# Moving sums from GpSimd to VectorE and multiplying one token tile plainly, in a Mamba-2 and mixer kernel

## The chip, the core and the metric

The kernel runs on one core of a Trainium2 chip. The core has a matrix engine (TensorE, "PE" in the profile; its weight loads are "PEld"), three engines for elementwise work (VectorE "DVE", ScalarE "ACT", GpSimd "POOL"), and SyncE ("SP"), which here only issues DMA transfers. The engines run side by side, each works through its own instructions in program order, and they wait for each other by semaphores. The metric is the device time of one execution in microseconds.

## The reference

Two blocks follow each other. The first is a chunked state-space recurrence over 4 batches, 8 heads, 768 tokens, head width 32 and state width 16. The second mixes tokens with a rank-32 product and channels with a two-layer network of width 1024.

```python
# first block: per chunk c of 32 tokens
cum = np.cumsum(la, axis=-1)
L = np.exp(cum[:, :, :, None] - cum[:, :, None, :]) * causal
M = np.einsum('bhin,bhjn->bhij', Cc, Bc) * L
y_intra = np.einsum('bhij,bhjd->bhid', M, xc)
y_inter = np.einsum('bhin,bhnd->bhid', Cc, state) * np.exp(cum)[:, :, :, None]
y[:, :, sl] = y_intra + y_inter
Bx = np.einsum('bhjn,bhjd->bhjnd', Bc, xc) * decay_from_j[:, :, :, None, None]
state = decay_full[:, :, None, None] * state + np.sum(Bx, axis=2)
# heads are joined to (batch, 768, 256), then the second block
h = x.transpose(0, 2, 1) @ U @ V
u = x + h.transpose(0, 2, 1)
out = u + np.maximum(u @ w_ch1, 0.0) @ w_ch2      # w_ch1: 256 x 1024, w_ch2: 1024 x 256
```

The weights of the second block come as 64-bit floats and everything else as 32-bit floats.

## The kernel before

The tokens of a batch are taken as 6 blocks of 128, two blocks at a time: a *pair* k is two blocks of 128 tokens, and there are 12 pairs, 3 for each batch. All matrix products are fp32; the profile shows each as two TensorE passes.

For a pair the first block of the reference runs in these steps. `prep` scales B and C on VectorE into `BC`; `decayed` scales B on GpSimd into `bd`; `turn` transposes `BC` on TensorE and ScalarE copies it out; `gram` forms C times B, `mask` applies the causal mask on VectorE, `state` and `update` carry the state on (TensorE, VectorE, and GpSimd for `Sm`), `intra` and `inter` form y, `yout` copies it out, and `ytokens` transposes it into token order.

```python
def prep(k, c=0, n=2):
    ...
    nc.vector.tensor_tensor(out=st[k]["BC"]..., in0=bc_sb[k]..., in1=F..., op=ALU.mult)

def decayed(k, c=0, n=2):
    ...
    nc.gpsimd.tensor_tensor(out=st[k]["bd"]..., in0=bc_sb[k]..., in1=FD..., op=ALU.mult)

def ytokens(k, c, n):
    ...
    copy = nc.scalar.copy if b == 0 else nc.vector.tensor_copy
    behind.setdefault("part", copy(out=ytok[b]..., in_=t))
```

The weights arrive as pairs of 32-bit words and are turned into fp32 by `to_fp32`, whose five VectorE and two ScalarE operations are spread out by calls of `convert_ahead`.

PSUM tiles come from `bank`; where TensorE would otherwise stand idle, `fill(n)` asks the next `bank` for n products of the identity with itself, whose result is overwritten, and `warm(n)` does the same at the start.

```python
def bank(tag, *dims):
    t = psum.tile([P, *dims], FP32, tag=tag, name=tag, bufs=BANKS[tag])
    for _ in range(fills[0]):
        ...
        nc.tensor.matmul(out=flat[:, :n], lhsT=ident, rhs=ident[:, :n], start=True, stop=True)
    fills[0] = 0
    return t
```

In the mixer of batch 0 the first product of the channel network is plain (`up`: one 128-column slice m of w_ch1 for one half k of the tokens, 384 columns wide). In the other batches it runs in *quads*: seven products instead of eight for each 2x2 split, with sums of the operands (`t` and `ws`) and of the results.

The second product is done in `down(j)` for j = 0, 1, 2, each for two tiles of 128 tokens, in all batches with seven groups of 128-column products. It needs four sums of gT, formed in `sums`, and sums of the weights, `w2s`, formed by `operands`.

```python
def sums(lo=0, hi=NM // 2, which=range(4)):
    ...
    for v, (l, r, op) in enumerate((
            (A21, A22, ALU.add), (S[0], A11, ALU.subtract),
            (A11, A21, ALU.subtract), (A12, S[1], ALU.subtract))):
        if v in which:
            engine = nc.gpsimd if b and j == 0 and lo < 3 else nc.vector
            engine.tensor_tensor(out=S[v][:, lo:hi], in0=l[:, lo:hi], in1=r[:, lo:hi], op=op)

def times(name, tag, lhsT, rhs, start=True, u=None):
    ...
    for i in range(NM // 2):                       # four products of 128 columns
        nc.tensor.matmul(out=X[name], lhsT=lhsT[:, i], rhs=rhs[:, i], ...)

def p1(): ...; times("x", "x", blocks()[0][0], w2b[0][0]); kept("e", "x")
def p5(): times("y", "z", S[0], w2s[0]); kept("power", "y")
# p6, p3, p7, p2, p4: the other five; `added` joins two results on VectorE into o, `store` sends o off

work = [(w2s[0], w2b[0][1], w2b[0][0], ALU.subtract), ...,     # 4 of w2s
        (ws[:, 0], A[2], A[3], ALU.add), ...]                  # 4 of ws
def operands(n, engine):
    for _ in range(min(n, len(work))):
        out, l, r, op = work.pop(0)
        engine.tensor_tensor(out=out, in0=l, in1=r, op=op)     # 128 x 512 each
```

The order in which the pieces of the mixer are interleaved with the pairs is written out by hand:

```python
for _ in range(3):
    some(2)                    # two up products
    convert_ahead()
decays(others, "y"); keep(others)
prep(3); decayed(3)
some(2)
turn(3); convert_ahead()
some(2)
gram(3); state(3); mask(3); update(3)
prep(4); decayed(4)
some(2)
turn(4); convert_ahead()
plan[0].append(convert_ahead)
...
for k in range(NPR, last + 1):                     # NPR = 3
    b, q = divmod(k, NPR)
    pieces = plan[q] if q or b == 1 else []        # mixer of the batch before
    if k > NPR:
        tokens = [lambda: ytokens(k - 1, 0, 2)]
        if q:
            pieces = pieces[:4] + tokens + pieces[4:]
        else:
            late = downs
            project, mixed, ups, plan, downs, _ = mixer(b - 1)
            pieces = (late[:1] + tokens + late[1:7] + [project] + late[7:11] + [mixed]
                      + late[11:] + (plan[0] if k < last else []))
    ...
    prep(k + 2); decayed(k + 2)
    run(pieces)
    turn(k + 2)
    inter(k, 0); gram(k + 1); intra(k); state(k + 1); mask(k + 1); inter(k, 1); yout(k)
    update(k + 1)
    if k == NPR + 1:
        run(ahead)                                 # the four sums of batch 0, j = 0
    if k < 2 * NPR:
        operands((2, 2, 4)[k - NPR], nc.gpsimd)
```

`plan[q]` for batch 0 is: two up products; two up products; the seven groups of j = 0 and the sums for j = 1.

Of the kernel before, what the change touches and what calls it, by code (L numbers as in the profile page):

```python
# [20 lines left out]
def kernel(  # L21
# [27 lines left out]
    nc = tc.nc  # L49
# [26 lines left out]

    def bank(tag, *dims):
        t = psum.tile([P, *dims], FP32, tag=tag, name=tag, bufs=BANKS[tag])
        for _ in range(fills[0]):
            flat = t if len(dims) == 1 else t.rearrange(  # L80
                {2: "p a b -> p (a b)", 3: "p a b c -> p (a b c)"}[len(dims)])
            n = min(P, flat.shape[1])
            nc.tensor.matmul(out=flat[:, :n], lhsT=ident, rhs=ident[:, :n], start=True, stop=True)
        fills[0] = 0
        return t
# [126 lines left out]
    def warm(n, tag="w"):  # L212

        t = bank(tag, P)
        for _ in range(n):
            nc.tensor.matmul(out=t, lhsT=ident, rhs=ident, start=True, stop=True)  # L216
# [307 lines left out]

    def mixer(b):
# [123 lines left out]
        def down(j):  # L649
# [7 lines left out]
            def sums(lo=0, hi=NM // 2, which=range(4)):  # L657
# [8 lines left out]
                for v, (l, r, op) in enumerate((  # L666
                        (A21, A22, ALU.add), (S[0], A11, ALU.subtract),
                        (A11, A21, ALU.subtract), (A12, S[1], ALU.subtract))):
                    if v in which:
                        engine = nc.gpsimd if b and j == 0 and lo < 3 else nc.vector  # L670
                        engine.tensor_tensor(out=S[v][:, lo:hi], in0=l[:, lo:hi],  # L671
                                             in1=r[:, lo:hi], op=op)
# [73 lines left out]

            return sums, [p1, p5, p6, p3, p7, p2, p4]
# [5 lines left out]
        def step(j, v, lo=0, hi=NM // 2):  # L753
            return lambda: sums[j](lo, hi, (v,))
# [26 lines left out]
        return project, mixed, ups, plan, downs, [step(0, v) for v in range(4)]  # L781
# [32 lines left out]
    project, mixed, ups, plan, downs, ahead = mixer(0)  # L814
# [71 lines left out]
    for _ in range(3):  # L886
        some(2)
        convert_ahead()
# [3 lines left out]
    decayed(3)  # L892
    some(2)
# [7 lines left out]
    prep(4)  # L901
    decayed(4)
    some(2)
    turn(4)
    convert_ahead()
    plan[0].append(convert_ahead)
# [21 lines left out]
    for k in range(NPR, last + 1):  # L928
        b, q = divmod(k, NPR)
        pieces = plan[q] if q or b == 1 else []  # L930
        if k > NPR:
            tokens = [lambda: ytokens(k - 1, 0, 2)]
            if q:
                pieces = pieces[:4] + tokens + pieces[4:]
            else:
                late = downs
                project, mixed, ups, plan, downs, _ = mixer(b - 1)
                pieces = (late[:1] + tokens + late[1:7] + [project] + late[7:11] + [mixed]
                          + late[11:] + (plan[0] if k < last else []))
# [58 lines left out]
```

## Time and profile before

| | |
|---|---|
| time, median of 3 runs | 256.12 us (255.63 to 256.95) |
| span of the profiled execution | 253.7 us |
| mean granted TensorE clock | 0.992 |
| down products of 128 columns (L682) | 275 to 287 ns each as recorded |
| quad products of 384 columns (L579) | 486 to 516 ns each as recorded |
| sums of 128x512 on VectorE (L671) | 0.69 to 1.75 us |
| operands of 128x512 on GpSimd (L922) | 1.26 to 1.72 us |

A line of the profile names a source line, an engine, an operation, and what it writes and reads. TensorE's passes overlap, so a recorded duration is longer than the distance from one start to the next: eight passes of 128 columns appear in the chain with 0.89 us, four of 384 columns with 1.29 us. The numbers of source lines are those of the kernel before: L359 is `turn`, L331 `prep`, L343 `decayed`, L377 `gram`, L389 `mask`, L436 `Sm`, L519 and L522 `ytokens`, L579, L588 and L622 the quads, L642 `up`, L671 `sums`, L682 and L696 `down`, L922 `operands`.

### The profile page before, as it was taken

How to read it: one execution, taken by the hardware profiler on the slowest of the kernel's cores; microseconds unless marked ns; L12 is line 12 of the kernel's file. 1: busy time of each engine (PE TensorE's matmuls, PEld its weight loads, DVE VectorE, ACT ScalarE, POOL GpSimd, SP SyncE). 2: the span in 40 equal slices, each digit the busy share in tenths (PEclk: the TensorE clock that was granted, in tenths of full speed). 3: DMA queues.
4: the chain of work that ended last, by engine and by line, in shares of the span. 5: the costliest groups of instructions: out<-in, count | busy, mean ns of one | idle time of the engine just before them, and what ended most of it. 6: DMA issues, size and time to landing. Idle time of an engine off the chain costs nothing.

```text
span 253.7 us, 7506 instructions
## 1 busy us (share of the span) xinstructions
PE 234.6 (92%) x3222; PEld 180.9 (71%) x3222; DVE 151.9 (60%) x337; ACT 96.1 (38%) x248; POOL 50.3 (20%) x74
## 2 busy tenths in 40 slices
PE   7988689797978979999989999999999999999995
PEld 7866556454768868656579979565599986558995
DVE  3366579969697986257584935265582462447521
ACT  5345457557521301347532301536522113563110
POOL 4031000103471480004270200005320000051000
PEclk9999799999999999999999999999999999999999
DMA  6989796999875401100000110100001011000111
GB/s 79 113 120 285 126 276 118 128 111 102 99 97 64 88 1 44 41 0 4 0 5 0 48 40 4 41 3 1 3 3 44 3 41 41 3 0 0 41 45 41
DMA packets 81637, 14.60 MB, mean 58 GB/s; under 512 B 76036, under 2 KB 79556, under 8 KB 81604
## 3 DMA queue, kind: packets, MB, share of 16 engines
q1 hardware_dynamic: 81604, 14.13, 30.9%
q8 instruction: 25, 0.41, 0.7%
q14 instruction: 8, 0.07, 0.1%
HBM read 10.98 MB, written 3.15 MB: 56 GB/s over the span
## 4 chain that ended last, share of the span: by engine, by line
PE 77%; DVE 13%; ACT 4%; issue 3%; DMA 1%; POOL 0%; DVEq 0%; SPq 0%; POOLq 0%; ACTq 0%
PE x L682 16%; PE x L579 12%; PE z L682 11%; PE z L579 8%; PE y L498 4%; DVE words L671 3%; PE y L478 3%; PE x L216 2%; PE w L359 2%; PE w L537 2%; PE w L519 2%; PE x L377 2%; DVE yT L552 1%; PE x L548 1%; PE w L409 1%
## 5 line engine op out<-in xcount | busy, mean ns | idle before, releaser
L579 PE MATMUL x<-t,ws 128*128 128x384 f32 x72 | 29.2, 503 | 0.5 <-ACT top L584 0.5
L436 POOL TENSOR_TENSOR Sm<-S,slot 128x256 f32<-128x256 f32 (+1 forms) x12 | 9.8, 813 | 99.2 <-DVE S L429 83.3
L682 PE MATMUL x<-w2s,words 128*128 128x128 f32 x192 | 25.5, 275 | 0.0
L682 PEld LDWEIGHTS x<-w2s,words 128*128 128x128 f32 x192 | 23.6, 193 | 0.1
L579 PEld LDWEIGHTS x<-t,ws 128*128 128x128 f32 x72 | 12.4, 189 | 13.5 <-ACT top L584 4.9
L740 ACT COPY o<-x 128x128 f32<-128x128 f32 x12 | 3.2, 266 | 45.9 <-PE x L682 45.9
L567 ACT ACTIVATE gT<-gT 128x384 f32<-128x384 f32 x36 | 17.6, 523 | 5.9 <-DVE gT L588 5.3
L671 POOL TENSOR_TENSOR words<-gT 128x256 f32<-128x256 f32 (+1 forms) x12 | 8.2, 682 | 48.4 <-PE x L579 36.3
L671 DVE TENSOR_TENSOR words<-gT 128x512 f32<-128x512 f32 (+1 forms) x20 | 16.8, 839 | 0.6 <-ACT gT L567 0.6
L389 DVE TENSOR_TENSOR M<-x,causal 128x256 int32<-128x256 int32 x24 | 10.1, 420 | 11.5 <-PE z L377 11.4
L343 POOL TENSOR_TENSOR bd<-bc,FD 128x256 f32<-128x256 f32 (+1 forms) x13 | 9.9, 772 | 29.9 <-ACT FD L264 29.9
L682 PE MATMUL x<-w,gT 128*128 128x128 f32 x96 | 14.0, 287 | 1.8 <-issue 1.1
L682 PEld LDWEIGHTS x<-w,gT 128*128 128x128 f32 x96 | 11.9, 191 | 4.6 <-DVE yT L552 2.5
L682 PE MATMUL z<-w,words 128*128 128x128 f32 x96 | 12.8, 276 | 1.9 <-DVE words L671 1.9
L588 DVE TENSOR_TENSOR gT<-z,top 128x384 f32<-128x384 f32 x12 | 6.7, 558 | 11.2 <-PE z L579 9.3
L622 DVE TENSOR_SCALAR gT<-x 128x384 f32<-128x384 f32 x12 | 6.7, 558 | 11.1 <-PE x L579 11.1
L510 ACT COPY yT<-y 128x256 f32<-128x256 f32 x24 | 7.8, 377 | 14.3 <-PE y L478 14.3
L682 PE MATMUL z<-w2s,words 128*128 128x128 f32 x96 | 12.7, 276 | 0.5 <-DVE words L671 0.5
L682 PEld LDWEIGHTS z<-w,words 128*128 128x128 f32 x96 | 11.7, 192 | 2.1 <-DVE words L671 2.1
L682 PE MATMUL z<-w,gT 128*128 128x128 f32 x96 | 12.7, 275 | 0.0
L682 PE MATMUL x<-w2s,gT 128*128 128x128 f32 x96 | 12.7, 275 | 0.0
L642 PE MATMUL x<-yT,w 128*128 128x384 f32 x32 | 12.0, 496 | 0.7 <-DVE yT L552 0.6
(159 smaller groups left out, 527.2 us busy)
## 6 DMA issues: line engine op xcount, KB each, us to landing
words<-in_moe_w_ch_dram SPq DMA_DIRECT2D x8, 512.0 KB, 6.3
x<-in_x_dram SPq DMA_DIRECT2D x24, 128.0 KB, 3.3
out_dram<-o SPq DMA_DIRECT2D x11, 256.0 KB, 2.1
bc<-in_B_dram SPq DMA_DIRECT2D x24, 64.0 KB, 3.8
bc<-in_C_dram SPq DMA_DIRECT2D x24, 64.0 KB, 3.3
words<-in_moe_U_dram SPq DMA_DIRECT2D x1, 192.0 KB, 4.9
words<-in_moe_V_dram SPq DMA_DIRECT2D x1, 192.0 KB
out_dram<-o SPq DMA_DIRECT2D x1, 128.0 KB, 1.7
```

What stands on the lines that cost most here:

```text
L343: nc.gpsimd.tensor_tensor(out=st[k]["bd"][:, c:c + n].rearrange("p c h n -> p (c h) n"), in0=bc_sb[k][:, 0, c:c + n].rearrange("p c h n -> ...
L389: done = nc.vector.tensor_tensor(out=M[:, r].bitcast(INT32).rearrange("p c s i -> p (c s) i"), in0=g[r].bitcast(INT32).rearrange("p c s i ...
L436: nc.gpsimd.tensor_tensor(out=s["Sm"][:, sl], in0=s["S"][:, sl].rearrange("p i (s d) -> p i s d", s=2), in1=slot[:, None, :, None].to_broa ...
L478: product = nc.tensor.matmul(out=y[p][ts(r % 2, H), r // 2, c], lhsT=own[ts(r, Q)], rhs=s["T"][ts(r, Q), 1, c, ts(p, H)], start=fresh(k, p ...
L498: nc.tensor.matmul(out=y[p][ts(i, Q), n, c], lhsT=x_sb[k][half, c, h], rhs=s["M"][half, h // 2, c, h % 2], start=fresh(k, p, [i]), stop=Tr ...
L510: nc.scalar.copy(out=yp[:, :, :, p], in_=st[k]["y"][p])
L567: nc.scalar.activation(g, g, AF.Relu)
L579: nc.tensor.matmul(out=X[name], lhsT=lhsT[:, ts(i, P)], rhs=rhs, start=start, stop=True, skip_group_check=True)
L588: nc.vector.tensor_tensor(out=g, in0=X[of], in1=X[other], op=ALU.add)
L642: nc.tensor.matmul(out=g, lhsT=w1[:, n, ts(m, P)], rhs=uT[:, n, ts(k, HS)], start=(n == 0), stop=(n == NCB - 1))
L671: engine.tensor_tensor(out=S[v][:, lo:hi], in0=l[:, lo:hi], in1=r[:, lo:hi], op=op)
L682: nc.tensor.matmul(out=X[name], lhsT=lhsT[:, i], rhs=rhs[:, i], start=start and u is None and i == 0, stop=True, skip_group_check=True)
```

## The change

The change does five things. All sums of gT run on VectorE, those of the quads' batches at later places in the order. The first two token tiles of batch 0 (j = 0) are multiplied plainly, with products of 256 columns and without sums. The operands `w2s` and `ws` move from GpSimd to VectorE. The fourth and fifth pair are scaled earlier, the up products and conversions that stood in the main loop move ahead of it. Fills of several products become one product over several copies of the identity. It is for taking work off GpSimd and for having the turns and the first down products wait for less. Beside that, tokens of batch 1 are copied by ScalarE instead of VectorE.

```diff
+    def idle(t, n):
+        while n > 0:
+            m = min(n, max(t.shape[1] // P, 1), 4)
+            w = min(P, t.shape[1])
+            nc.tensor.matmul(out=t[:, :m * w].rearrange("p (m i) -> p m i", i=w), lhsT=ident,
+                             rhs=ident[:, None, :w].to_broadcast([P, m, w]), start=True, stop=True)
+            n -= m
     def bank(tag, *dims):
-        for _ in range(fills[0]):
-            ... nc.tensor.matmul(out=flat[:, :n], lhsT=ident, rhs=ident[:, :n], ...)
+        if fills[0]:
+            idle(..., fills[0])
     def warm(n, tag="w"):
-        t = bank(tag, P)
-        for _ in range(n):
-            nc.tensor.matmul(out=t, lhsT=ident, rhs=ident, start=True, stop=True)
+        idle(bank(tag, 4 * P), n)
@@ ytokens
-        copy = nc.scalar.copy if b == 0 else nc.vector.tensor_copy
+        copy = nc.scalar.copy if b < 2 else nc.vector.tensor_copy
@@ sums
-                        engine = nc.gpsimd if b and j == 0 and lo < 3 else nc.vector
-                        engine.tensor_tensor(...)
+                        nc.vector.tensor_tensor(...)
@@ down
+            def whole(k):
+                g = bank("x", DM)
+                for n in range(NCB):
+                    nc.tensor.matmul(out=g[:, ts(n, P)], lhsT=uT[:, n, ts(HT * k + j, P)],
+                                     rhs=ident, is_transpose=True, ...)
+                for half in range(2):
+                    for i in range(NM // 2):
+                        m = half * NM // 2 + i
+                        nc.tensor.matmul(out=g, lhsT=blocks()[k][half][:, i], rhs=w2[:, m], ...)
+                to(k, 0)
+                behind.setdefault("part", nc.scalar.copy(out=hold["o"][:, k], in_=g))
+                if k:
+                    store(None, None)
+                    del hold["o"]
+            if b == 0 and j == 0:
+                return sums, [lambda: whole(0), lambda: whole(1)]
@@ mixer
-            plan = [[ups.pop(-2), ups.pop()], [ups.pop(-2), ups.pop()], downs.pop(0)]
+            plan = [[ups.pop(-2), ups.pop()]] + [[piece] for piece in downs.pop(0)]
             plan[2] += [step(1, v) for v in range(4)]
         elif b < NB - 1:
             for v in range(4):
-                plan[1].insert(2 * v, step(0, v, 0, 2))
-                plan[1].append(step(0, v, 2, 4))
+                plan[1].insert(6 + 2 * v, step(0, v, 0, 2))
+            plan[1] += [step(0, v, 2, 4) for v in range(4)]
@@ before the main loop
-    for _ in range(3):
+    for _ in range(2):
         some(2)
         convert_ahead()
     decays(others, "y"); keep(others)
     prep(3); decayed(3)
+    some(2); convert_ahead()
+    some(2); convert_ahead()
+    prep(4); decayed(4)
     some(2)
     turn(3); convert_ahead()
     some(2)
     gram(3); state(3); mask(3); update(3)
-    prep(4); decayed(4)
+    convert_ahead()
     some(2)
     turn(4)
-    convert_ahead()
-    plan[0].append(convert_ahead)
@@ main loop
-                pieces = pieces[:4] + tokens + pieces[4:]
+                pieces = pieces[:3] + tokens + pieces[3:]
-                          + late[11:] + (plan[0] if k < last else []))
+                          + late[11:] + [lambda: operands(4, nc.vector)] + (plan[0] if k < last else []))
-        if k == NPR + 1:
-            run(ahead)
-        if k < 2 * NPR:
-            operands((2, 2, 4)[k - NPR], nc.gpsimd)
+        if k < NPR + 2:
+            operands(2, nc.vector)
```

More of the change, by code (lines that the diff above doesn't have):

```diff
@@ L75 @@
     fills = [0]
+    def idle(t, n):
[5 more added lines that the diff above has]
+            n -= m
     def bank(tag, *dims):
         t = psum.tile([P, *dims], FP32, tag=tag, name=tag, bufs=BANKS[tag])
-        for _ in range(fills[0]):
[L80 to L83, printed above, removed]
+        if fills[0]:
+            idle(t if len(dims) == 1 else t.rearrange(
+                {2: "p a b -> p (a b)", 3: "p a b c -> p (a b c)"}[len(dims)]), fills[0])
         fills[0] = 0
@@ L669, in sums @@
                     if v in which:
-                        engine = nc.gpsimd if b and j == 0 and lo < 3 else nc.vector
-                        engine.tensor_tensor(out=S[v][:, lo:hi], in0=l[:, lo:hi],
-                                             in1=r[:, lo:hi], op=op)
+                        nc.vector.tensor_tensor(out=S[v][:, lo:hi], in0=l[:, lo:hi],
+                                                in1=r[:, lo:hi], op=op)
             def times(name, tag, lhsT, rhs, start=True, u=None):
@@ L745, in p4 @@
                 del hold["o"]
+            def whole(k):
+                g = bank("x", DM)
+                for n in range(NCB):
+                    nc.tensor.matmul(
+                        out=g[:, ts(n, P)], lhsT=uT[:, n, ts(HT * k + j, P)], rhs=ident,
+                        is_transpose=True, start=(n == 0), stop=False, skip_group_check=True)
+                for half in range(2):
+                    for i in range(NM // 2):
+                        m = half * NM // 2 + i
+                        nc.tensor.matmul(out=g, lhsT=blocks()[k][half][:, i], rhs=w2[:, m],
+                                         start=False, stop=(m == NM - 1), skip_group_check=True)
+                to(k, 0)
[5 more added lines that the diff above has]
+                return sums, [lambda: whole(0), lambda: whole(1)]
             return sums, [p1, p5, p6, p3, p7, p2, p4]
@@ L780, in mixer @@
         downs = [piece for pieces in downs for piece in pieces]
-        return project, mixed, ups, plan, downs, [step(0, v) for v in range(4)]
+        return project, mixed, ups, plan, downs
     halves = [half for w in weights for half in (to_fp32(*w),) * 2]
@@ L813 @@
     ytok[0] = mix.tile([P, NC, DM], FP32, tag="ytok", name="ytok")
-    project, mixed, ups, plan, downs, ahead = mixer(0)
+    project, mixed, ups, plan, downs = mixer(0)
     decays(one)
@@ L892 @@
     decayed(3)
+    some(2)
+    convert_ahead()
+    some(2)
+    convert_ahead()
+    prep(4)
+    decayed(4)
     some(2)
@@ L900 @@
     update(3)
-    prep(4)
-    decayed(4)
+    convert_ahead()
     some(2)
     turn(4)
-    convert_ahead()
-    plan[0].append(convert_ahead)
+    assert not halves
     ws = const.tile([P, 5, DF // 2], FP32)
@@ L933 @@
             if q:
-                pieces = pieces[:4] + tokens + pieces[4:]
+                pieces = pieces[:3] + tokens + pieces[3:]
             else:
                 late = downs
-                project, mixed, ups, plan, downs, _ = mixer(b - 1)
+                project, mixed, ups, plan, downs = mixer(b - 1)
                 pieces = (late[:1] + tokens + late[1:7] + [project] + late[7:11] + [mixed]
-                          + late[11:] + (plan[0] if k < last else []))
+                          + late[11:] + [lambda: operands(4, nc.vector)] + (plan[0] if k < last else []))
         if k == last:
```

## The prediction

> **What bounds the kernel now.** I read the page's busy times and chain first, then the stretches, then the timeline wherever TensorE stands still.
>
> ```profile
> PE 234.6 (92%) x3222; PEld 180.9 (71%) x3222; DVE 151.9 (60%) x337; ACT 96.1 (38%) x248; POOL 50.3 (20%) x74
> ...
> PE 77%; DVE 13%; ACT 4%; issue 3%; DMA 1%; POOL 0%; DVEq 0%; SPq 0%; POOLq 0%; ACTq 0%
> ```
>
> TensorE is the bound and the chain is 77% TensorE. What can be won without removing products is the 13% of VectorE and the 3% of "issue". Where those lie is seen by stretch (columns: PE, PEld, DVE, ACT, POOL busy us, then clock, DMA share, GB/s):
>
> ```profile
> 34.00:56.00 22.00, 19.28 (x134) 11.50 (x133) 18.28 (x39) 13.29 (x29) 1.08 (x1) 1.00 0.90 162
> 56.00:77.00 21.00, 17.39 (x368) 12.44 (x367) 18.64 (x35) 10.49 (x25) 11.53 (x11) 1.00 0.83 100
> 77.00:94.00 17.00, 15.47 (x307) 14.30 (x308) 15.37 (x26) 3.31 (x10) 8.26 (x7) 1.00 0.30 47
> 104.00:130.00 26.00, 25.73 (x372) 14.98 (x370) 14.36 (x32) 14.18 (x33) 7.12 (x10) 1.00 0.04 12
> ```
>
> From 34 to 94 us VectorE is 83 to 90% busy and TensorE loses 2.7, 3.6 and 1.5 us. From 104 on TensorE is full (25.73 of 26) and VectorE half empty. So the change can pay before 94 us, and its extra VectorE work has room after that. TensorE's stops, one by one, in the timeline (in brackets: idle time and what ended it):
>
> ```profile
> 49.55 0.63 PE L359 MATMUL w<-ident,BC 128*128 128x128 f32 x4 [1.90 <-ACT gT L647]
> 62.13 0.63 PE L359 MATMUL w<-ident,BC 128*128 128x128 f32 x4 [1.27 <-DVE BC L331]
> ...
> 72.85 1.71 POOL L922 TENSOR_TENSOR w2s<-w 128x512 f32<-128x512 f32 x1
> 73.36 1.75 DVE L671 TENSOR_TENSOR words<-gT 128x512 f32<-128x512 f32 x1
> 75.03 1.74 DVE L671 TENSOR_TENSOR words<-gT,words 128x512 f32<-128x512 f32 x1
> 76.83 1.16 PE L682 MATMUL z<-w,words 128*128 128x128 f32 x8 [1.85 <-DVE words L671]
> ...
> 82.00 0.69 DVE L671 TENSOR_TENSOR words<-gT 128x512 f32<-128x512 f32 x1
> ...
> 93.91 0.33 PE L678 MATMUL x<-ident,t 128*128 128x128 f32 x1 [1.30 <-DVE o L696]
> ...
> 131.16 1.05 PE L682 MATMUL x<-w,gT 128*128 128x128 f32 x7 [1.15 <-issue]
> ```
>
> The reader is to see that one and the same sum takes VectorE 0.69 us at 82.00, when GpSimd rests, and 1.75 us at 73.36, when GpSimd forms an operand (1.71 us). TensorE's waits at 76.83 and 93.91 both lie behind such stretched sums. The waits at 49.55 and 62.13 are turns (transposes) of the fourth and sixth pair; their scaled BC comes late because it queues on VectorE behind weight conversions. Taking start to start against the usual pitch of each matmul, TensorE loses 2.06 us before the turn at 49.55, 1.44 before 62.13, 2.80 between 71.9 and 76.8, 0.39 at 85.6 and 1.46 at 93.9: 8.15 us in all. That is what the change can reach.
>
> [...]1.75 us beside GpSimd, 0.69 us alone, nearly the sum of both operations. [...]The page's instruction queue has 25 packets with 0.41 MB[...] the packet from 128.58 to 129.81 us stands right before the "issue" stop that ends at 131.16.
>
> **The change part by part.**
>
> *Scaling sooner.* The fourth pair is now scaled three groups of up products ahead of its turn, the fifth ahead of the fourth's turn, and all conversions end before the main loop. One more group of up products (two halves, 8 passes of 0.323 us, 2.58 us) runs before the fifth pair's turn. That only moves TensorE work. I follow both engines from 35.66 us. TensorE: two groups to 40.9, decays (1.45) to 42.35, three groups to 50.1, turn to 50.6, a group to 53.1, gram and state to 55.1. VectorE: a conversion takes 2.6 us; conversions to 45.3, kept and scaling to 46.7, two conversions and the fifth pair's scaling to 53.2 (0.8 of it lost to GpSimd's two bd products), a conversion to 55.8, mask to 57.1, update to 58.3, last conversion (three operations) and scaling to 61.6. The seventh group needs a bank that the mask frees at 56.25, so it ends at 58.85; turn and the next group end at 61.9, when the sixth pair's scaling is just ready. Before, that turn began at 62.13 with one group fewer. Gain 0.2 + 2.6 = 2.8 us of the 3.5 us lost there.
>
> *First token tile plainly.* Removed: 56 passes of 128 columns at 0.112 us (0.89 us for 8 in the chain), 6.27 us. Added: 2 x 8 products of 256 columns, 32 passes; midway between 0.112 and the 384 columns' 0.323 us that is 0.2175 each, 6.96 us. TensorE pays 0.7 us. But the four first sums (0.69 + 0.88 + 1.75 + 1.75 = 5.1 us of VectorE) are gone, and with them the 2.80 us stop.
>
> *Operands on VectorE.* Eight operations at 0.69 us, 5.5 us, replace eight of 1.3 to 1.7 us on GpSimd. Two each follow the updates of two rounds, ahead of the scaling that a turn waits for, and overlap GpSimd's Sm and bd (0.9 + 1.0 us)[...]. I put 0.35 us of waiting on each of those two turns, 0.7. The four ws stand at the end of the third round, where VectorE is idle 2.7 us; the first is needed 0.6 us after the quads begin, the fourth 2.6 us after. Nothing lost there.
>
> Round by round: the turn at 61.9, pair work to 64.95, whole product (3.5 + 0.2) to 68.65, tokens and turn with the wait to 69.85, pair work to 72.3, second whole product to 76.0, tokens and turn with the wait to 77.2, pair work to 79.7. There the second token tile begins; before, it began at 84.21. So 4.5 us are won by then (2.8 + 2.8 - 0.7 - 0.7 and 0.3 of small stops). After it the stretched sums are gone: 0.39 + 1.46 = 1.85 us more. Together 6.35 us.
>
> *Sums on VectorE in the other batches.* 24 operations leave GpSimd, 20 of 128x256 and 4 of 128x128. At 0.34 us, the pitch of the mask of 128x256, and 0.2 us for the small ones (estimated from that), they add 7.6 us to a VectorE that is about half idle there. In the last batch four in a row (1.4 us) fall into a VectorE gap of 1.37 us at 222.75. I count no loss. The tokens' later place and the relieved ScalarE may remove two stops of 0.42 us (119.6, 174.7); I count half, 0.4.
>
> *Merged fills.* The columns stay. 13 instead of 18 fills and 4 instead of 12 warm products leave 26 passes fewer, 52 instructions with their weight loads; the plain tile saves 48 more. At 0.112 us per pass with the same columns this is worth nothing by itself. It moves the 256-instruction borders. The stop at 131.16 (1.42 us with its pitch) falls on such a border after a burst of short matmuls; the new borders fall into other bursts, two or three of them with a whole block inside. I count 1.42 won and about 1.1 lost: 0.3.
>
> Sum: 6.35 + 0.4 + 0.3 = 7.05. 256.1 - 7.1 = 249.0 us.
>
> **The rivals.** *VectorE stays the bound before 62 us.* It was 83% busy from 34 to 56, and nothing of that work is removed, only reordered; if each conversion is stretched by GpSimd more than I allowed (in the profile, at 57.4 to 61.3, one took 3.9 us instead of 2.6), the earlier scaling only exchanges one wait for another, and 2 us of the gain go: 251. For it: my slack there is 0.3 us. Against: the removed sums come later and VectorE catches up. *The fetch becomes the new wait.* If three bursts meet a border badly, at 1.2 us each, and the one at 131 is gone, 2 us are lost: 251. If none does: 248. *The sums on VectorE block TensorE's banks.* VectorE's adds free the z and x banks in the quads; if each of 24 sums delays one by 0.1 to 0.2 us, 3 us are lost: 252. Against: VectorE idles 0.7 to 1.4 us between adds there. *Fully hidden relief*: my slips (about 1.7 us) do not occur and the small stops vanish: 246.5.
>
> **Range and chances.** Each rival alone costs about 2 to 3 us, two together bring it near 252; the good case gives 246.5. The 2% line is at 251.0, 2 us above my value; about one in five outcomes lies beyond it, and slower by 2% would need a cost that no stretch of the profile shows.
>
> **What would show it.** Right: no wait of 1 us or more at the turns of the fourth to sixth pair; TensorE's share above 94%; the 128x512 sums near 0.7 us; GpSimd with Sm and bd only; the second token tile's products 4 to 5 us earlier, the second batch's first quad 6 to 7. Wrong: waits on BC at the turns of the seventh and eighth pair, "issue" stops above 1 us inside the bursts of short matmuls, or waits of TensorE on gT adds in the quads.

## The result and the profile after

| | before | after |
|---|---|---|
| time, median of 4 runs | 256.53 us (255.63 to 258.85) | 249.17 us (248.27 to 250.53) |
| span of the profiled execution | 253.7 us | 246.5 us |

The ratio is 0.9704, 95% interval [0.9622, 0.9786]: 3.0% less time. The predicted 249.0 us lies 0.2 us from the median. Whether that is so for the reasons given is another question, and part of it is not.

From the page of the kernel after: busy times, granted clock, chain.

```profile
PE 233.2 (95%) x3172; PEld 177.1 (72%) x3172; DVE 153.8 (62%) x359; ACT 97.6 (40%) x249; POOL 22.9 (9%) x42
...
PEclk9999889999999999999999999999999999999999
...
PE 82%; DVE 10%; ACT 4%; issue 3%; POOL 0%; DVEq 0%; POOLq 0%; ACTq 0%
```

TensorE has 1.4 us less work and 5.8 us less idle time. In the chain VectorE's share fell from 13 to 10%, TensorE's rose from 77 to 82%, and "issue" is still 3%. (Line numbers of after: L364 is `turn`, L336 `prep`, L382 `gram`, L414 `state`, L675 `sums`, L686 and L700 `down`, L761 the plain product, L950 `operands`, L584 and L593 the quads.) The stretches that were shown of before, now of after (PE, PEld, DVE, ACT, POOL busy us, then clock, DMA share, GB/s):

```profile
34.00:56.00 22.00, 20.36 (x137) 12.29 (x138) 20.69 (x41) 14.94 (x33) 1.65 (x2) 1.00 0.91 161
56.00:77.00 21.00, 21.00 (x428) 16.59 (x428) 16.82 (x36) 10.02 (x24) 5.89 (x6) 1.00 0.92 108
77.00:94.00 17.00, 15.62 (x273) 14.05 (x264) 11.46 (x25) 4.05 (x13) 1.96 (x2) 1.00 0.22 51
104.00:130.00 26.00, 25.88 (x411) 18.29 (x411) 19.70 (x47) 12.07 (x29) 3.42 (x4) 1.00 0.01 3
```

From 56 to 77 us TensorE now has no gap at all, and VectorE has room there. Before 56 us VectorE is busier than it was (20.69 of 22 us) and TensorE still loses 1.6. After 77 us the loss is 1.4 us, although VectorE is only 67% busy: something else ends a wait there. TensorE's timeline of after names them (in brackets: idle time and what ended it):

```profile
49.86 0.60 PE L364 MATMUL w<-ident,BC 128*128 128x128 f32 x4
...
54.31 0.32 PE L382 MATMUL x<-Cm,T 32*64 32x128 f32 x1 [0.91 <-ACT gT L652]
...
61.58 0.60 PE L364 MATMUL w<-ident,BC 128*128 128x128 f32 x4
...
64.74 3.62 PE L761 MATMUL x<-w,gT 128*128 128x256 f32 x16
...
79.34 0.35 PE L414 MATMUL w<-x,bd 64*32 64x64 f32 x17 [1.17 <-issue]
80.01 1.16 PE L686 MATMUL x<-w,gT 128*128 128x128 f32 x8
```

The turns (L364) wait for nothing any more. In their place stands one wait of 0.91 us for ScalarE inside the grams (L382). The plain product (L761) runs without a stop. And at 79.34, in the state products (L414), there is a new "issue" stop of 1.17 us, just before the second token tile begins at 80.01.

The table below divides the span by four events of TensorE's timeline: the first up product, the first product of the second token tile of batch 0, and the first quads of batches 1, 2 and 3. Lengths are in us from the event before.

| kernel | first up at | to second tile | to quad 1 | to quad 2 | to quad 3 | to the end | up to end |
|---|---|---|---|---|---|---|---|
| before | 35.66 | 48.55 | 19.20 | 55.08 | 52.83 | 42.36 | 218.0 |
| after | 35.45 | 44.55 | 17.27 | 53.69 | 52.53 | 42.99 | 211.0 |
| won | 0.2 | 4.0 | 1.9 | 1.4 | 0.3 | -0.6 | 7.0 |

### The profile page after: what moved, and what is told of

It reads as the page before. It is cut to its first block, busy times and chain, and to the rows that moved or that the text cites. A ratio compares the mean times of both kernels' runs of the same rounds, so it can differ in the third digit from the quotient of the medians.

```text
span 246.5 us, 7386 instructions
## 1 busy us (share of the span) xinstructions
PE 233.2 (95%) x3172; PEld 177.1 (72%) x3172; DVE 153.8 (62%) x359; ACT 97.6 (40%) x249; POOL 22.9 (9%) x42
## 4 chain that ended last, share of the span: by engine, by line
PE 82%; DVE 10%; ACT 4%; issue 3%; POOL 0%; DVEq 0%; POOLq 0%; ACTq 0%
PE x L686 17%; PE x L584 13%; PE z L686 12%; PE z L584 9%; PE y L503 3%; PE y L483 3%; PE x L761 3%; PE w L542 3%; PE w L524 2%; PE x L82 2%; DVE words L675 2%; PE w L364 2%; PE x L382 2%; DVE yT L557 1%; PE w L414 1%
## 5 line engine op out<-in xcount | busy, mean ns | idle before, releaser
L584 PE MATMUL x<-t,ws 128*128 128x384 f32 x72 | 29.2, 503 | 0.6 <-DVE gT L593 0.5
L686 PE MATMUL x<-w2s,words 128*128 128x128 f32 x176 | 23.2, 275 | 0.0
L584 PEld LDWEIGHTS x<-t,ws 128*128 128x128 f32 x72 | 12.3, 189 | 12.9 <-ACT top L589 4.3
L686 PEld LDWEIGHTS x<-w2s,words 128*128 128x128 f32 x176 | 21.6, 193 | 0.0
L675 DVE TENSOR_TENSOR words<-gT 128x512 f32<-128x512 f32 (+2 forms) x30 | 17.4, 579 | 0.6 <-ACT gT L572 0.6
L503 PE MATMUL y<-M,x 64*32 64x64 f32 x768 | 10.8, 224 | 3.2 <-issue 2.7
L686 PE MATMUL x<-w,gT 128*128 128x128 f32 x88 | 12.6, 285 | 0.6 <-DVE yT L557 0.6
L686 PEld LDWEIGHTS x<-w,gT 128*128 128x128 f32 x88 | 10.8, 191 | 3.2 <-DVE yT L557 2.5
L503 PEld LDWEIGHTS y<-M,x 64*32 64x32 f32 x768 | 8.5, 105 | 5.4 <-issue 4.4
L434 DVE SCALAR_TENSOR_TENSOR S<-S,kept,w 128x64 f32<-128x64 f32 x40 | 11.2, 279 | 1.7
L593 DVE TENSOR_TENSOR gT<-z,top 128x384 f32<-128x384 f32 x12 | 6.7, 558 | 8.8 <-PE z L584 8.8
L647 PE MATMUL z<-yT,w 128*128 128x384 f32 x32 | 11.6, 486 | 0.0
L686 PE MATMUL x<-w2s,gT 128*128 128x128 f32 x88 | 11.6, 275 | 0.0
L686 PE MATMUL z<-w,words 128*128 128x128 f32 x88 | 11.6, 275 | 0.0
## 6 DMA issues: line engine op xcount, KB each, us to landing
out_dram<-o SPq DMA_DIRECT2D x11, 256.0 KB, 2.1
```

The source lines that it names most:

```text
L434: done = nc.vector.scalar_tensor_tensor(out=new, in0=st["S", b], scalar=kept[:, b, j, None], in1=add, op0=ALU.mult, op1=ALU.add)
L503: nc.tensor.matmul(out=y[p][ts(i, Q), n, c], lhsT=x_sb[k][half, c, h], rhs=s["M"][half, h // 2, c, h % 2], start=fresh(k, p, [i]), stop=Tr ...
L584: nc.tensor.matmul(out=X[name], lhsT=lhsT[:, ts(i, P)], rhs=rhs, start=start, stop=True, skip_group_check=True)
L647: nc.tensor.matmul(out=g, lhsT=w1[:, n, ts(m, P)], rhs=uT[:, n, ts(k, HS)], start=(n == 0), stop=(n == NCB - 1))
L675: nc.vector.tensor_tensor(out=S[v][:, lo:hi], in0=l[:, lo:hi], in1=r[:, lo:hi], op=op)
```

## The experiments

Names that begin with a_ are edits of the kernel after, b_ of the kernel before. A ratio is against the kernel before on the same chip. One execution of a kernel differs from the next by up to some us, mostly ahead of the first up product (see the last section), so where a part of the change is weighed, lengths of stages from the profile decide. Most of that difference goes with the mean granted clock: in 27 executions the kernel before took 253.7 to 254.1 us at 0.998 or more, 254.7 to 256.8 at 0.992 or 0.993, 256.0 to 257.0 at 0.986 or 0.987, and 257.6 to 260.1 at 0.979 or 0.980. For after and a_again together these are 246.8 to 248.2, 248.3 to 249.1, 249.7 to 250.5 and, once, 252.9 us. Where whole times are compared below, the clock is named. The profiled executions of a_shift, a_words5 and b_tok were among the longer ones of their kernels (mean clock 0.972, 0.985 and 0.980), with TensorE at half clock for a few us in one of the stages read, so their stages are used only where that does not touch them.

The stages of all experiments:

| kernel | first up at | to second tile | to quad 1 | to quad 2 | to quad 3 | to the end | up to end |
|---|---|---|---|---|---|---|---|
| a_late | 34.02 | 49.22 | 17.27 | 53.91 | 52.53 | 43.00 | 215.9 |
| b_plain | 37.54 | 46.27 | 19.27 | 53.66 | 53.58 | 42.35 | 215.1 |
| a_pool_ops | 35.33 | 43.59 | 18.11 | 53.88 | 52.61 | 42.98 | 211.2 |
| a_pool_tok | 37.03 | 43.61 | 19.35 | 53.68 | 52.53 | 42.99 | 212.2 |
| b_tok | 37.34 | 50.32 | 17.98 | 55.37 | 52.86 | 42.34 | 218.9 |
| a_fills | 36.99 | 44.65 | 17.27 | 53.40 | 52.52 | 42.98 | 210.8 |
| a_shift | 41.71 | 46.34 | 17.27 | 53.43 | 52.53 | 42.98 | 212.5 |
| a_best | 37.93 | 44.85 | 18.91 | 53.40 | 52.53 | 42.34 | 212.0 |
| a_pool_sums | 36.12 | 44.56 | 17.27 | 54.58 | 52.75 | 42.35 | 211.5 |
| a_last | 35.09 | 44.58 | 17.27 | 53.92 | 52.54 | 42.36 | 210.7 |
| a_again | 33.65 | 44.59 | 17.27 | 53.68 | 52.53 | 42.98 | 211.1 |
| a_words5 | 35.59 | 46.81 | 17.27 | 53.93 | 52.54 | 42.35 | 212.9 |

### The earlier scaling, undone

a_late puts scaling, conversions and up products back to their places of before; all else is as after. In the first lines `one` and `two` are the two plain products.

```diff
-            plan = ... + [[piece] for piece in downs.pop(0)]
+            one, two = downs.pop(0)
+            plan = [[ups.pop(-2), ups.pop()], [ups.pop(-2), ups.pop(), one], [two]]
@@ before the main loop
-    for _ in range(2):
+    for _ in range(3):
         some(2); convert_ahead()
     decays(others, "y"); keep(others)
     prep(3); decayed(3)
-    some(2); convert_ahead()
-    some(2); convert_ahead()
-    prep(4); decayed(4)
     some(2)
     turn(3); convert_ahead()
     some(2)
     gram(3); state(3); mask(3); update(3)
-    convert_ahead()
+    prep(4); decayed(4)
     some(2)
-    turn(4)
+    turn(4); convert_ahead()
+    plan[0].append(convert_ahead)
```

> The changed kernel with the scaling of the fourth and fifth pair, the up products and the conversions at the places of the kernel before (two up products stand ahead of the first plain product). Theory: the stops of 2.06 and 1.44 us at the turns of the fourth and sixth pair return and the time is 2.3 to 3.0 us above the changed kernel (ratio to before 0.979 to 0.982). Rival, VectorE is the bound before 62 us in both orders and the order only moves a wait: within 0.5 us of the changed kernel (ratio 0.970 to 0.972).

Measured: 252.42 us, ratio 0.9890 [0.9849, 0.9930]. TensorE's stops in its timeline:

```profile
47.89 0.63 PE L364 MATMUL w<-ident,BC 128*128 128x128 f32 x4 [1.88 <-ACT gT L652]
...
60.47 0.63 PE L364 MATMUL w<-ident,BC 128*128 128x128 f32 x4 [1.28 <-DVE BC L336]
...
64.98 0.55 PE L414 MATMUL w<-x,bd 64*32 64x64 f32 x28 [2.15 <-issue]
```

Both stops of before are back to within 0.02 us, so this reordering as a whole cures them and nothing else of the change does; scaling, conversions and up products were not taken apart. From first up to the sixth pair's turn takes 26.45 us (60.47 - 34.02), as in before (62.13 - 35.66 = 26.47). In after it takes 26.13 us with one group of up products, 2.58 us, more. The earlier scaling is thus worth 0.3 + 2.6 = 2.9 us. To the second tile a_late loses more, 4.6 us against a_again (49.22 - 44.59). The rest, 1.7 us, is "issue": start to start, 2.36 us before 64.98 and 0.58 in a later burst, against 1.27 in a_again. The expectation was missed by just that part. It is not equally large in every execution: at a clock of 0.993 a_late took 4.1 to 5.2 us more than after and a_again, at 0.986 only 1.2 to 2.8; why was not traced.

### The plain token tile alone

b_plain gives the kernel before the whole(0) and whole(1) of after, and no first four sums.

```diff
+            def whole(k): ...                      # as in the change
+            if b == 0 and j == 0:
+                return sums, [lambda: whole(0), lambda: whole(1)]
-        if k == NPR + 1:
-            run(ahead)
```

> The kernel before with the first token tile of batch 0 multiplied plainly and its four sums left away; nothing else. Theory: TensorE pays 0.7 us for the wider products and wins the 2.8 us of stops between 71.9 and 76.8, so the time is about 2.1 us below the kernel before (ratio 0.990 to 0.994); the stop of 1.3 us at 93.9 stays. Rival, [...]the stop comes back at the second tile, because its four sums now meet the operands on GpSimd, and the time is equal or up to 0.7 us more (ratio 1.000 to 1.003).

Measured: 252.83 us, ratio 0.9891 [0.9836, 0.9946]. The second tile begins 46.27 us after the first up, 2.3 us sooner than before. The waits at L682 (0.62 and 2.01 us, start to start) are gone with the products that waited. The product itself costs TensorE what was worked out: 32 passes at 0.216 us are 6.91 us, for 6.27 us removed. The wait ahead of L678 (93.91 in before) is still there, which shows that the plain tile has no part in it:

```profile
93.58 0.33 PE L678 MATMUL x<-ident,t 128*128 128x128 f32 x1 [1.29 <-DVE o L696]
```

The "issue" stop of before at 131.16 is gone here too, without merged fills: fewer instructions ahead of it are enough. That gives 1.4 us on the way to quad 2; 0.75 us of it are lost again before quad 3, where a wait of 0.21 us at 179.66 and an "issue" stop of 0.34 us at 185.09 are new.

### Operands back on GpSimd

```diff
-                          + late[11:] + [lambda: operands(4, nc.vector)] + (plan[0] if k < last else []))
+                          + late[11:] + (plan[0] if k < last else []))
-        if k < NPR + 2:
-            operands(2, nc.vector)
+        if k < 2 * NPR:
+            operands((2, 2, 4)[k - NPR], nc.gpsimd)
```

> The changed kernel with the eight operands on GpSimd at the places of the kernel before. [...]the 128x512 sums of the second and third token tile take 1.5 to 1.8 us again instead of 0.7 to 1.0, TensorE waits over 1 us for VectorE between 74 and 92 us, and the time is 1.5 to 2.5 us above the changed kernel (ratio to before 0.976 to 0.980). Rival, the plain tile alone relieved VectorE[...]: no TensorE wait above 0.3 us there, ratio 0.970.

Measured: 248.22 us, ratio 0.9708 [0.9664, 0.9751], that is, nothing lost. Lines of its timeline:

```profile
75.35 1.76 DVE L675 TENSOR_TENSOR words<-gT 128x512 f32<-128x512 f32 x1
...
80.44 0.63 PE L524 MATMUL w<-ident,yT 128*128 128x128 f32 x4 [0.37 <-ACT e L692]
...
83.83 1.76 DVE L675 TENSOR_TENSOR words<-gT 128x512 f32<-128x512 f32 x1
85.00 1.72 POOL L950 TENSOR_TENSOR ws<-w 128x512 f32<-128x512 f32 x1
```

And of the timeline of after:

```profile
72.91 0.99 DVE L950 TENSOR_TENSOR w2s<-w,w2s 128x512 f32<-128x512 f32 x1
...
74.85 0.68 DVE L675 TENSOR_TENSOR words<-gT 128x512 f32<-128x512 f32 x1
...
81.56 1.10 DVE L675 TENSOR_TENSOR words<-gT 128x512 f32<-128x512 f32 x1
```

The sums are stretched again: 1.76 us beside operands on GpSimd that take 1.61 to 1.72 us, against 0.68 at 74.85 in after. But with the plain tile no product waits for them for long; TensorE stops for under 0.4 us at a time. Second tile to first quad costs 0.84 us more than after. On the other side the "issue" stop of after at 79.34 is not seen in this profile, where a wait of 0.39 us for the mask stands near it, and the stage before is 1.0 us shorter. This theory of mine, that this stretching alone would cost 1.5 to 2.5 us of the time, fell. Beside GpSimd's Sm and bd, which remain, a sum takes 0.99 to 1.10 us: 0.3 to 0.4 us of delay instead of 1.06.

### The copies of tokens

a_pool_tok is a_pool_ops with the tokens of batch 1 copied by VectorE, as in before. b_tok is before with only that copy on ScalarE.

```diff
 a_pool_tok
-        copy = nc.scalar.copy if b < 2 else nc.vector.tensor_copy
+        copy = nc.scalar.copy if b == 0 else nc.vector.tensor_copy
 b_tok
-        copy = nc.scalar.copy if b == 0 else nc.vector.tensor_copy
+        copy = nc.scalar.copy if b < 2 else nc.vector.tensor_copy
```

> The changed kernel with the eight operands on GpSimd, as in an earlier run, and also the three token copies of batch 1 on VectorE instead of ScalarE. If only both loads together made VectorE late at the second token tile in the kernel before, the stop of about 1.4 us before the transpose of t comes back: 1.0 to 1.5 us above the run with the operands alone (ratio to before 0.975 to 0.977). Rival, the plain tile lets VectorE reach the second tile early enough for both: no TensorE wait above 0.6 us for VectorE there, ratio 0.970 to 0.972.

> The kernel before with the three token copies of batch 1 on ScalarE instead of VectorE and nothing else. Theory: VectorE is 0.7 us less late at the second token tile, so the stop of 1.46 us at 93.9 us shrinks by 0.6 to 0.8 us and that at 85.6 goes; second tile to first quad 18.2 to 18.5 us instead of 19.2, ratio to before 0.995 to 0.998. Rival, [...]the stop keeps 1.3 us or more.

Measured: a_pool_tok 250.20 us, ratio 0.9705 [0.9632, 0.9778]; b_tok 254.95 us, ratio 0.9970 [0.9940, 0.9999]. In a_pool_tok the old wait is back:

```profile
90.48 0.33 PE L682 MATMUL x<-ident,t 128*128 128x128 f32 x1 [1.30 <-DVE o L700]
```

Second tile to first quad goes from 18.11 to 19.35 us, the 19.20 of before. The ratio hides it, because the clocks differ: at 1.000 a_pool_tok took 247.7 and 248.1 us and a_pool_ops 246.2, at 0.992 or 0.993 they took 249.4 and 247.8 to 248.7. In b_tok the same stage goes from 19.20 to 17.98 us and that wait disappears altogether, where I expected only part of it to go; the small one of 0.39 us at L519 stays. At a clock of 0.992 or 0.993 the median of 11 executions of b_tok is 254.47 us and of 12 of before 255.76, 1.3 us more. What was moved stands in VectorE's queue of before right ahead of the stretched sums:

```profile
86.28 0.69 DVE L522 COPY ytok<-w 128x512 f32<-128x512 f32 x1
86.89 1.73 DVE L671 TENSOR_TENSOR words<-gT 128x512 f32<-128x512 f32 x1
```

In b_tok the copy's 0.69 us are gone from there, and the first sum, which then begins 0.52 us ahead of GpSimd's operand instead of 0.09 behind it, takes 1.10 us. So, in both kernels, the copy is worth 1.2 us and the operands some 0.8. The half sentence at the end of the change's description carries more than the operands.

### The merged fills and the instruction borders

Counting TensorE's records (matmuls, weight loads and its semaphore instructions, by their starts), every "issue" stop above 0.3 us in all these profiles stands at record 195 + 256 n or the one before it:

| kernel | record: time, idle us |
|---|---|
| before | 963: 27.62, 2.45; 3779: 131.16, 1.15 |
| after | 963: 27.89, 2.68; 2499: 79.34, 1.17 |
| a_late | 963: 27.76, 2.64; 1731: 64.98, 2.15; 2498: 82.57, 0.37 |
| a_fills | 963: 27.56, 2.33; 2243: 74.59, 1.18 |
| b_plain | 963: 28.65, 3.74; 5314: 185.09, 0.34 |
| a_shift | 707: 26.70, 2.35; 2499: 87.04, 1.06 |

TensorE has 6498 records in before and 6397 in after, that is, 25 such borders in each, and q8 of the page's "instruction" queues has 25 packets in each (0.41 MB, 16384 bytes a packet in the trace). I call such a packet a block. Most borders pass without a stop: of the 25, two in before and two in after have one above 0.3 us. In after, the transfer of a block runs from 77.00 to 77.95 us, and the stop ends 1.4 us later. Records 2338 to 2497 start while it runs: the burst of small products comes to its last record before the stop 1.75 us after the border (2243 at 76.20). That TensorE waits there for the block is my reading of these times. In every stop of the table TensorE goes on 1.3 to 1.5 us after the end of a transfer; at 64.98 in a_late that transfer (62.47 to 63.45) began 6.4 us after the border before it (56.12). A border is not enough for a stop: a_pool_ops passes record 2499 without one. Two experiments move the count.

a_fills makes the merged fills and warm products separate again:

```diff
-        while n > 0:
-            m = min(n, max(t.shape[1] // P, 1), 4)
-            ... out=t[:, :m * w] ..., rhs=ident[:, None, :w].to_broadcast([P, m, w])
-            n -= m
+        for _ in range(n):
+            nc.tensor.matmul(out=t[:, :w], lhsT=ident, rhs=ident[:, :w], start=True, stop=True)
```

> The changed kernel with fills and warm products as separate products again: 26 passes, 52 TensorE instructions more. Theory of instruction borders: the stop of 1.17 us at 79.34 lies on the border between two 256-instruction blocks inside a burst of short matmuls; 52 instructions more put that border 52 places earlier in the program, into the slow plain products, so the next block is there in time. Expected: no issue stop above 0.5 us between 60 and 90 us, time 1.0 to 1.3 us below the changed kernel (ratio to the kernel before 0.965 to 0.967); the stop near 25 us stays. Rival, merging saves TensorE time by itself: up to 1 us above the changed kernel, and the stop at 79 us stays where it is.

Measured: 250.34 us, ratio 0.9808 [0.9755, 0.9860]. The stop at 79 is gone as expected, but not the loss. It now stands in the transposes that open the second plain product:

```profile
74.59 0.33 PE L752 MATMUL x<-ident,yT 128*128 128x128 f32 x1 [1.18 <-issue]
```

From first up to end it takes 210.8 us, after 211.0: the merged fills are worth nothing there. The greater time comes from ahead of the first up product (36.99 against 35.45), where TensorE ran 6.8 us at half clock in this execution. At a clock of 0.986 a_fills took 249.1 and 249.9 us, after and a_again 249.7 to 250.5, so at the same clock it is not slower; whether separate fills make half clock more frequent was not separated.

a_shift puts nine products of eight columns behind the first warm products of after, to move the borders by 36 records.

```diff
     warm(3, "x")
+    tiny = bank("x", P)
+    for _ in range(9):
+        nc.tensor.matmul(out=tiny[:, :8], lhsT=ident, rhs=ident[:, :8], start=True, stop=True)
```

> The changed kernel with nine products of the identity with its first 8 columns added behind the first warm products: 36 TensorE instructions more and nothing else. Theory of instruction borders: stops named issue stand at instruction 193 plus a multiple of 256[...]. 36 instructions more put the border of the stop at 79 us into slow products; no stop above 0.6 us between 60 and 200 us, time 0.9 to 1.4 us below the changed kernel (ratio to before 0.964 to 0.967). Rival, the stop belongs to the state products it stands in and not to the count: it stays at those products and the ratio stays at 0.970.

Measured: ratio 0.9755 [0.9669, 0.9842], from two executions of 250.36 and 250.49 us at a clock of 1.000; the other four took 254.87 to 256.30 us at 0.972 to 0.980. The stop stays at record 2499, now in the intra products at 87.04 instead of the state products: it goes by the count and not by what is multiplied there. My estimate that the transfer would then fit between the bursts was wrong: the border before it (81.31) lay 4.7 us ahead of the stop, but the block came only from 84.71 to 85.65. And the nine products were not free: at a clock of 1.000 a_shift takes 3.5 us more than a_again, and its first turn begins at 11.3 us, in the kernels without them at 6.7 to 7.7 (see the last section).

### Sums in the quads' batches

a_pool_sums returns the sums of batches 1 to 3 to GpSimd and to their old places, and with them the tokens of the quads. a_last is after with GpSimd only for the first sums of the last batch. a_best is a_shift and a_last together.

```diff
 a_pool_sums
-                        nc.vector.tensor_tensor(out=S[v][:, lo:hi], ...)
+                        engine = nc.gpsimd if b and j == 0 and lo < 3 else nc.vector
+                        engine.tensor_tensor(out=S[v][:, lo:hi], ...)
-                plan[1].insert(6 + 2 * v, step(0, v, 0, 2))
-            plan[1] += [step(0, v, 2, 4) for v in range(4)]
+                plan[1].insert(2 * v, step(0, v, 0, 2))
+                plan[1].append(step(0, v, 2, 4))
-                pieces = pieces[:3] + tokens + pieces[3:]
+                n = 3 if b == 1 else 4
+                pieces = pieces[:n] + tokens + pieces[n:]
 a_last
-                        nc.vector.tensor_tensor(out=S[v][:, lo:hi], ...)
+                        engine = nc.gpsimd if b == NB - 1 and j == 0 and lo < 3 else nc.vector
+                        engine.tensor_tensor(out=S[v][:, lo:hi], ...)
```

> The changed kernel with the first sums of batches 1 to 3 back on GpSimd at the places of the kernel before, tokens too. Theory: this part of the change gives and takes. Two stops of 0.42 us at the tokens of the quads return, the stop of 0.7 us in the last batch goes, and the time is within 0.5 us of the changed kernel (ratio to before 0.969 to 0.972). Rival, moving the sums to VectorE is worth more than 1.5 us by itself: ratio 0.976 or more.

> The changed kernel with the first sums of the last batch (all but the last quarter) back on GpSimd and nothing else. Theory: TensorE's stop of 0.7 us near 218 us goes; from the last batch's first quad to the end 42.3 us instead of 43.0, and the time 0.6 to 0.7 us below the changed kernel, which the ratio can only just show. Rival, [...]the same 43.0 us.

> The same 36 instructions, and in the last batch alone the first sums (all but the last quarter) back on GpSimd, as in the kernel before. If the four sums in a row on VectorE make TensorE wait 0.7 us near 218 us, that stop goes as well: ratio to before 0.961 to 0.964, 0.6 to 0.8 us below the run with the 36 instructions alone. Rival, the stop at 218 us is the bank wait of the quads whatever the engine: no difference from the run with the 36 instructions alone.

Measured: a_pool_sums 247.95 us, ratio 0.9653 [0.9591, 0.9715]; a_last 247.60 us, ratio 0.9703 [0.9661, 0.9745]; a_best 252.73 us, ratio 0.9842 [0.9780, 0.9904].

In a_pool_sums the two stops of 0.43 us at the quads are back (114.9 and 168.7 us) and the last batch ends 0.6 us sooner; from first up to end it takes 0.5 us more than after, with an "issue" stop of 0.51 us at 110.79 that after does not have. The move gives and takes; its total is within the spread. What it takes is seen in the last batch of after, here with both engines:

```profile
216.30 0.56 DVE L593 TENSOR_TENSOR gT<-z,top 128x384 f32<-128x384 f32 x1 [1.37 <-PE z L584]
216.77 0.42 DVE L675 TENSOR_TENSOR words<-gT 128x256 f32<-128x256 f32 x1
217.22 0.43 DVE L675 TENSOR_TENSOR words<-words,gT 128x256 f32<-128x256 f32 x1
217.57 0.42 DVE L675 TENSOR_TENSOR words<-gT 128x256 f32<-128x256 f32 x1
217.90 0.42 DVE L675 TENSOR_TENSOR words<-gT,words 128x256 f32<-128x256 f32 x1
218.24 0.55 DVE L593 TENSOR_TENSOR gT<-z,e 128x384 f32<-128x384 f32 x1
```

VectorE's gap of 1.37 us is there, but the sums come behind the add that ends it, and hold up the next two adds, which free banks, by 1.5 us. TensorE's quad at 219.31 waits for that:

```profile
219.31 1.56 PE L584 MATMUL x<-t,ws 128*128 128x384 f32 x4 [0.54 <-DVE gT L593]
```

a_last takes these sums off VectorE: the stop is gone and the last stage takes 42.36 us instead of 42.98. a_best, expected at a ratio of 0.961 to 0.964, has this gain too (42.34) but pays the nine products at the start, and after its own "issue" stop TensorE ran at half clock from 82.9 to 86.3 us:

```profile
81.76 0.30 PE L506 MATMUL y<-M,x 64*32 64x64 f32 x2 [1.34 <-issue]
82.77 1.99 PE L690 MATMUL x<-w,gT 128*128 128x128 f32 x8
```

The same eight passes take 1.16 us in after. Second tile to first quad grows by 1.6 us.

### The kernel after again, and a last step

a_again is the kernel after unchanged. a_words5 is a_last with five buffers instead of six for the words of the weights and the sums of gT.

```diff
-NWORDS = 6
+NWORDS = 5
```

> The changed kernel itself once more, as the measure for the two runs beside it. Expected: ratio to before 0.967 to 0.975, 211 us from the first up product to the end; before the first up product 34 to 37.5 us, by the number of 3.4 us pieces at half the TensorE clock that follow the stop at 25 us.

> The run with the last batch's sums on GpSimd, and five instead of six buffers for the weight words, so that one 512 KB load leaves the busy stretch from 17 to 28 us and comes later. Theory: the instruction block that TensorE waits for at 25 us queues behind data loads (4.6 us from the border before it to the transfer's start); with a quarter less ahead of it the stop shrinks from 2.5 to about 1.5 us, fewer pieces at half clock follow, and the time is 1 to 2 us lower than the run beside it. Rivals: the load that was put off makes the conversions wait (up products after 42 us stop for VectorE, 1 to 2 us higher), or the stop has another cause and keeps its 2 to 3 us.

Measured: a_again 248.62 us, ratio 0.9713 [0.9655, 0.9771]; a_words5 246.66 us, ratio 0.9618 [0.9559, 0.9678]. a_words5 has the shortest time of all kernels here. Why is open: in its profile the stop at 28 us that it was to shorten is still 2.53 us, with the block's transfer beginning at 25.6 us as in the others. At a granted clock of 0.998 or more, a_words5 has spans of 243.0 to 246.1 us and a_again 244.7 to 246.0. Of that difference the last batch's sums explain 0.6 us; the rest was not traced. The kernel before has 252.0 to 252.3 us at such a clock, so 7 us separate before and after there too.

a_again shows how much one execution is worth. Its profile and that of after have the same stages to within 0.05 us from the first up product on (211.05 and 211.02 us); the spans differ by 1.8 us, all of it ahead of it; the first up product came at 33.65 us, a little before the 34 to 37.5 expected. The row of its granted clock:

```profile
PEclk9999999999999999999999999999999999999999
```

And that of a_fills, with two 7s where after has two 8s:

```profile
PEclk9999779999999999999999999999999999999999
```

## Why the prediction was right, point by point

**The bound.** Right. TensorE's share went from 92 to 95%, and the gain lies where it was sought: 5.9 of 7.2 us between the first up product and the first quad of batch 1. The signs named for being right came: no wait of 1 us at the turns, the second tile 4.2 us and the first quad of batch 1 6.1 us earlier. Of the three signs named for being wrong two came as well: an "issue" stop above 1 us inside a burst (1.17 us at 79.34) and a wait of TensorE on a gT add in the quads (0.54 us at 219.31). So the parts that were to bring most held, and those at the borders and in the later batches did not.

**Scaling sooner: 2.8 us predicted, 2.9 measured.** The sixth pair's turn was put at 61.9 and came at 61.58. The wait before it was put on the bank that the mask frees; it was ScalarE's gT at the grams, 0.91 us at 54.31. The place was wrong, the size near enough. The rival "VectorE stays the bound before 62 us" did not come about, though VectorE is 94% busy before 56 us.

**The plain tile: 2.8 - 0.7 = 2.1 predicted, 2.3 measured** by b_plain.

**Operands on VectorE: a loss of 0.7 us predicted at two turns, none measured.** The operand and the scaling beside Sm and bd took 0.99 and 1.10 us, which VectorE had in hand. This step was wrong, too cautious.

**Second tile: 79.7 predicted, 80.01 measured.** The 0.7 us not lost at the turns, and more, went into the "issue" stop of 1.38 us (start to start) at 79.34.

**The stretched sums after it: 1.85 us predicted, 1.93 measured, 1.2 of it for a reason that was not named.** The prediction put all of it on sums stretched beside GpSimd. The profiles show the stretching, 1.76 us in a_pool_ops against 0.68 in after; but a stretched sum is a cost only where a product waits for it. a_pool_ops puts 0.8 us on the operands; a_pool_tok and b_tok put 1.2 us on the copy of tokens, which the prediction counts nowhere; it even speaks of "the relieved ScalarE", while the copies come to ScalarE (busy 96.1 us before, 97.6 after). The failed step was to read the releaser at 93.91, "DVE o", as late because of the sums ahead of it, without asking what else VectorE had in its queue there.

**Later batches: 0.4 predicted.** Both stops of 0.42 us are gone, 0.84 in all. But where no loss was counted, the last batch loses 0.63 us, and at 123.14 and 176.53 TensorE gets its next products 0.31 and 0.36 us late, because VectorE begins the masks only behind four moved sums (the last of them starts at 122.33, the first mask at 122.66); a_pool_sums has neither of these two waits. Together about -0.5. The failed step is "I count no loss": the gap of 1.37 us ends with the add that comes ahead of the four sums, not behind them.

**Fills and borders: +0.3 predicted.** The stop at 131.16 is gone (1.42 us), as said. New at borders are 1.38 us at 79.34 and 0.22 us at 109.62: 1.6 in all, where 1.1 was counted. So about -0.2 us instead of +0.3. a_fills shows that this is no property of the merged fills: with them undone one stop goes and one comes.

The sum: 7.05 us predicted; 0.2 + 4.0 + 1.9 + 1.4 + 0.3 - 0.6 = 7.2 in the profiles. The prediction was too hopeful by 0.5 us in the borders and by 0.9 in the later batches, too cautious by 0.7 at the turns, and some 0.6 us of the 7.2 belong to none of the parts weighed here. That all this cancelled to 0.2 us is luck.

## What to carry to other kernels

Moving work off an engine paid here only where a product waited for it: look up who waits for each stretched instruction and what else stands in that queue before the gain is put on one cause. A sum meant for an engine's gap has to stand ahead of the instruction that ends the gap; that order was not run here, but behind it the sums cost 0.6 us. Where bursts of small matmuls met a border of 256 records, TensorE stopped in some of these profiles, for 0.3 to 2.2 us after the first up product, and edits ahead in the program moved that stop (a_fills to record 2243, a_shift to the intra products at 87.04), so keep it apart when a small change is judged.

## What the hardware showed that I had not expected

**Instruction borders cost up to 3.7 us.** For the stop at 28 us of after, at a DMA share of 0.90, the block comes from 25.45 to 26.49 us, 4.9 us after the border before it (20.56), while all of TensorE's records up to 961 had already started; the same stop was 1.57 us in a_pool_ops and 3.74 in b_plain. In before, at a DMA share of 0.04, the block for 131.16 came 1.0 us after the border (127.62 to 128.58), and the idle time was 1.15 us. That data loads hold the block up is argued from this, not shown: before 79.34 the share was 0.77 (74 to 80 us) and the block came after 0.8 us, and a_words5, with a load fewer, kept its stop.

**Half clock in pieces of 3.41 us.** Where the traces of before and after have a granted clock, it is 1.0 or 0.5, and the one whole piece at 0.5 lasts 3.413 us in each (from 27.86 us in before, from 29.47 in after). Over all profiles: within the stop at 28 us or up to 1.6 us behind it, one piece of 3.41 us at 0.5 begins in before, after, a_pool_ops, a_pool_sums, a_last and a_words5, two in a row in a_fills, b_plain, a_pool_tok and b_tok, none in a_late and a_again. First up is then at 35.1 to 36.1, at 37.0 to 37.5, and at 33.7 to 34.0 us. The length of a stop alone does not decide it: a piece followed a stop as short as 1.34 us (a_best) and, 2 us later, waits of 0.93 and 1.13 us (a_shift, a_words5), but none followed stops of 2.12 (a_again) and 2.64 us (a_late). One such piece lowers the mean clock of 250 us by 0.007, so the steps of the clock between executions, 1.000, 0.993, 0.986 and 0.979, fit none, one, two and three pieces; a step takes 0.6 to 1.9 us in the medians of before. What starts a piece, and why it changes from one execution to the next, was not shown.

**Small products with full weights were not small here.** Nine products of eight columns are 18 passes with weights of 128x128. In a_best, as in a_shift, they run from 2.87 us until the next product starts at 6.57:

```profile
2.87 3.85 PE L227 MATMUL x<-ident 128*128 128x8 f32 x18
6.57 0.56 PE L232 MATMUL w<-ident,a_sb 96*128 96x96 f32 x2
```

That is 3.70 us, 0.21 us a pass, before full clock is granted. In the same early stretch of before a pass of 128 columns takes 0.23 to 0.25 us (six from 1.43 to 2.94, four from 3.31 to 4.21), so sixteen times fewer columns saved hardly anything here. The first turn comes 3.5 to 4.6 us later than in the other kernels; what is not the passes themselves, up to 0.9 us, goes with the full clock, which is granted from 11.2 or 11.3 us instead of 5.5 to 8.0. What in a pass takes the time was not separated.
